# Pair 3's transposes moved from TensorE to the DMA crossbar, and the loads held differently

## The chip, the cores and the metric

The kernel runs on one core of one Trainium2 chip. A core has five engines that run their own instruction streams and wait for each other through semaphores: TensorE (PE, matmuls, with its weight loads listed apart as PEld), VectorE (DVE), ScalarE (ACT), GpSimd (POOL) and SyncE (SP), and 16 DMA engines that move data between memory and the core. The metric is device time in microseconds for one execution; lower is better. Six runs of the kernel before gave 228.18 to 228.51 us, median 228.28 us.

## The reference: what is computed

A gated recurrence over 768 tokens for 4 batches and 8 heads of width 64, followed by a feed-forward layer with a sigmoid gate:

```python
gamma = 1.0 - 2.0 ** (-5.0 - np.arange(H))
scale = 1.0 / np.sqrt(D)
for t in range(S):
    state = gamma[None, :, None, None] * state + np.einsum('bhd,bhe->bhde', k[:, :, t], v[:, :, t])
    y[:, :, t] = scale * np.einsum('bhd,bhde->bhe', q[:, :, t], state)
x = y.transpose(0, 2, 1, 3).reshape(B * S, H * D)          # 3072 x 512
gate = 1.0 / (1.0 + np.exp(-(x @ w_gate)))                 # d_ff 1536
out = gate * (x @ w_val) @ w_out                           # 3072 x 512
```

## The kernel before

**Tiles and stages.** The recurrence is computed in chunks of C = 128 tokens. There are NT = 6 chunks; the four batches of a chunk are treated as two *pairs* of batches, so there are 12 pairs, numbered i = 2t + h for chunk t and batch half h. Pairs 0 and 1 (chunk 0) form the start of the kernel and have code of their own (`first_...`). For a later pair the steps are:

- `load_kq(i)` (L69): k and q of the pair come as bf16 into tiles `kn[i]` and `qn[i]`, three DMA issues each (L63 once, L67 twice: the second batch has its heads swapped two by two). `load_v(i)` (L54) brings `vs[i]` in one issue (L57). All of these are issued by POOL and converted from float32 on the way. `load_next(i)` (L488) is `load_kq` and `load_v`, seven issues.
- k and q must stand with the head width on the partitions for the score matmuls. This is done in one of two ways. `transpose(i, j)` (L203) transposes eight 128x128 blocks on PE into a bank of PSUM (L207) and has ACT copy them to the tile `kqT[i]` (L208); j is the batch of the pair. `xbar(i)` (L210) has SP issue two transposing DMAs, one for k and one for q (L213), into a tile of the tag `kqX` (four buffers). The kernel before transposes pairs 2 and 3 on PE and pairs 4 to 11 by the DMA crossbar.
- `scale_k(i)` (L216, L218): POOL multiplies `kn[i]` by a table of decays, giving `ks[i]`.
- `scores` (L226), `mask` (L232, DVE, with the table `maskk`), `inter` (L242: the old state times q), `intra` (L249: the masked scores times v), `y_out` (L265, DVE, into `xT[t]`, the input of the feed-forward layer), `state` (L272: `ks` times v), `state_sum` (L281) and `casts` (L285). `block(old, new)` (L287) does `inter`, `intra` and `y_out` of one pair and `scores`, `state` and `mask` of the next.

The feed-forward layer works on a chunk's 512 tokens: `up` (L386) has PE compute a gate part and a value part (L364), ACT takes the sigmoid (L382) and DVE the product (L383); `down` (L394) has PE multiply with `wo` (L399), ACT copy the result (L403) and SP issue the output's DMA (L404), 256 KB for each of the four batches of a chunk.

**What sets the order.** The schedule is written out by hand: each engine's queue takes its instructions in the order in which the program states them, and only semaphores hold them back. An instruction of an engine therefore waits behind everything that the program gave to this engine earlier. Chunk 0's feed-forward layer is written out (L468 to L521), with pair 2's and part of pair 3's steps between its parts. For t = 1 to 5 the loop at L542 goes through the groups of `up` and `down` of that chunk (20 groups: in chunk 1 six groups for each half of the tokens, then eight groups of `down`; in chunks 2 to 5 twelve of `up` and eight of `down`), and after a group does the steps that the dictionary `plan` (L530) names for it. A step `(4, xbar, 4)` under 1 is done after group 4 of chunk 1.

**The hold.** `hold(i)` (L527, L528) has POOL copy one element of pair i's transposed q into a small tile. The result is used by nobody; the copy makes POOL wait for the crossbar transfer of q, and so everything that POOL does after it, loads above all, comes after that transfer.

**The constants.** `last_constants` (L174) has DVE make a 0/1 mask in `causal`; `later_tables` (L177) has POOL build `tabsk` (L182, four copies) and `maskk` (L184, two products), which `scale_k` and `mask` need.

Of the kernel before, what the change touches and what calls it, by code (L numbers as in the profile page):

```python
# [9 lines left out]
BF16 = mybir.dt.bfloat16  # L10
# [5 lines left out]
def kernel(  # L16
# [12 lines left out]
    nc = tc.nc  # L29
# [3 lines left out]
    C = 128  # L33
    NT = S // C
    NP = H // 2
# [7 lines left out]
    const = ctx.enter_context(tc.tile_pool(name="const", bufs=1))  # L43
# [6 lines left out]
    kn, qn, ks, vs, kqT = {}, {}, {}, {}, {}  # L50
# [3 lines left out]
    def load_v(i):  # L54
        t, h = divmod(i, 2)
        vs[i] = ld.tile([C, 2 * H, D], BF16, tag="vs", name="vs", bufs=6)
        nc.gpsimd.dma_start(out=vs[i], in_=v[2 * h:2 * h + 2, :, t * C:(t + 1) * C, :].rearrange("b h s d -> s (b h) d"))  # L57
# [11 lines left out]
    def load_kq(i):  # L69
        load_swapped(kn, k, i, "kn", 6)  # L70
        load_swapped(qn, q, i, "qn", 4)
# [13 lines left out]
    def load_out(s):  # L85
        nc.gpsimd.dma_start(out=wo[:, s * 3:(s + 1) * 3, :],
                            in_=moe_w_out.rearrange("(n p) d -> p n d", p=128)[:, s * 3:(s + 1) * 3, :])
# [86 lines left out]
    def last_constants():  # L174
        nc.vector.tensor_scalar(causal, ahead, 0.0, None, op0=ALU.is_le)

    def later_tables():  # L177
        src = tabs.rearrange("s (p e) t -> s e t p", e=2)
        dst = tabsk.rearrange("s t j (p e) -> s j e t p", e=2)
        for j in range(2):  # L180
            for e in range(2):
                nc.gpsimd.tensor_copy(dst[:, j, e], src[:, e ^ j])  # L182
        for e in range(2):
            nc.gpsimd.tensor_tensor(maskk[:, e], causal.unsqueeze(1).to_broadcast([128, NP, C]),  # L184
                                    tabsk[:, 0, e, 0::2].unsqueeze(2).to_broadcast([128, NP, C]), op=ALU.mult)
# [5 lines left out]
    def bank(shape, dt=F32):  # L191
        return pf.tile(shape, dt, tag="ff", name="ff")

    def half(e):
        return slice(e * D, (e + 1) * D)

    def heads(t, j, p):
        return t[:, j * H + 2 * p:j * H + 2 * p + 2, :].rearrange("s h d -> s (h d)")

    def new_kqT(i):  # L200
        kqT[i] = at.tile([128, 2, 2, NP, C], BF16, tag="kqT", name="kqT", bufs=2)

    def transpose(i, j):  # L203
        tp = bank([128, 2, NP, C], BF16)
        for which, x in enumerate((kn[i], qn[i])):
            for p in range(NP):
                nc.tensor.transpose(tp[:, which, p, :], heads(x, j, p), ident)  # L207
        nc.scalar.copy(kqT[i][:, :, j], tp)  # L208

    def xbar(i):  # L210
        kqT[i] = at.tile([128, 2, 2, NP, C], BF16, tag="kqX", name="kqX", bufs=4)
        for which, x in enumerate((kn[i], qn[i])):
            nc.sync.dma_start_transpose(out=kqT[i][:, which].rearrange("d j p s -> d (j p) s"),  # L213
                                        in_=x.rearrange("s h d -> s (h d)"))

    def scale_k(i):  # L216
        ks[i] = ld.tile([C, 2 * H, D], BF16, tag="ks", name="ks", bufs=3)
        nc.gpsimd.tensor_tensor(ks[i], kn[i], tabsk[:, i // 2].rearrange("s j h -> s (j h)").unsqueeze(2)  # L218
                                .to_broadcast([C, 2 * H, D]), op=ALU.mult)
# [14 lines left out]
    def new_y(i):  # L234
        for j in range(2):
            y[i, j] = bank([128, NP, C])
# [19 lines left out]
    def x_of(t, kk, lo=0, hi=512):  # L256
        per = NP // len(xT[t])
        return xT[t][kk // per][:, kk % per, lo:hi]
# [17 lines left out]
    def new_za(i):  # L276
        za[i] = at.tile([128, 2, NP, D], F32, tag="za", name="za", bufs=4)
# [5 lines left out]
    def casts(i):  # L283
        zb[i] = at.tile([128, 2, NP, D], BF16, tag="zb", name="zb", bufs=4)
        nc.vector.tensor_tensor(zb[i], za[i], tabz[:, i // 2 + 1].unsqueeze(3).to_broadcast([128, 2, NP, D]), op=ALU.mult)  # L285
# [58 lines left out]
    def first_state(i):  # L344
        z = bank([128, 2, NP, D])
        for j in range(2):
            for p in range(NP):
                for e in range(2):
                    n = j * H + 2 * p + e
                    nc.tensor.matmul(z[half(e ^ j), j, p, :], ks[i][:, n, :], vs[i][:, n, :],  # L350
                                     start=(j == 0 and p == 0), stop=True, skip_group_check=True)
        new_za(i)
        nc.vector.tensor_copy(za[i], z)
# [5 lines left out]
    def up_part(t, w, n1s, lo=0, hi=512):  # L359
        n = hi - lo  # L360
        u = bank([128, 512])
        for i, n1 in enumerate(n1s):
            for kk in range(KT):
                nc.tensor.matmul(u[:, i * n:(i + 1) * n], w[:, kk, n1 * 128:(n1 + 1) * 128], x_of(t, kk, lo, hi),  # L364
                                 start=(kk == 0), stop=(kk == KT - 1))
        return u[:, :len(n1s) * n]
# [9 lines left out]
    def gate_times_val(t, n1s, lo, hi, ps):  # L376
        n = hi - lo
        if t not in hT:
            hT[t] = ffn.tile([128, NFF, 512], BF16, tag="hT", name="hT", bufs=2)
        gs = ffn.tile([128, 512], F32, tag="gs", name="gs")  # L380
        g = gs[:, :len(n1s) * n]
        nc.scalar.activation(g, ps[0], AX.Sigmoid)  # L382
        nc.vector.tensor_tensor(hT[t][:, n1s[0]:n1s[-1] + 1, lo:hi], g.rearrange("p (i n) -> p i n", n=n),  # L383
                                ps[1].rearrange("p (i n) -> p i n", n=n), op=ALU.mult)
# [6 lines left out]
    def rows(t, b):  # L391
        return b * S + t * C

    def down(t, b, lo, hi):  # L394
        if lo == 0:
            po[b] = bank([128, 512])
        o = po[b]
        for n1 in range(lo, hi):
            nc.tensor.matmul(o, hT[t][:, n1, b * C:(b + 1) * C], wo[:, n1, :], start=(n1 == 0), stop=(n1 == NFF - 1))  # L399
        if hi < NFF:  # L400
            return
        ob = ffn.tile([128, D_MODEL], F32, tag="ob", name="ob")
        nc.scalar.copy(ob, o)  # L403
        nc.sync.dma_start(out=out[rows(t, b):rows(t, b) + C, :], in_=ob)  # L404
# [65 lines left out]
    for n1 in (2, 4):  # L470
        gates = [up_part(0, wg, (n1 + i,)) for i in range(2)]
        for i in range(2):
            gate_times_val(0, (n1 + i,), 0, 512, (gates[i], up_part(0, wv, (n1 + i,))))
        first_state(n1 // 2 - 1)
    last_constants()
    load_out(0)
    load_out(1)
    load_kq(2)
    load_out(2)
    later_tables()  # L480
    load_out(3)
    load_v(2)
    casts(0)
# [4 lines left out]
    def load_next(i):  # L488
        load_kq(i)
        load_v(i)  # L490

    load_next(3)
    scale_k(2)
    new_kqT(2)
# [10 lines left out]
        mask(2, j, 1)  # L505
    for b in range(3):
        down(0, b, 9, 12)
    load_next(4)
    down(0, 3, 0, 6)
    new_y(2)  # L510
    inter(2)
# [5 lines left out]
    state_sum(2)  # L517
    down(0, 3, 6, 12)
    casts(2)
    new_kqT(3)  # L520
    transpose(3, 0)  # L521

    held = const.tile([128, 1], BF16, name="held")

    def hold(i):  # L527
        nc.gpsimd.tensor_copy(held, kqT[i][:, 1, 1, NP - 1, C - 1:C])  # L528

    plan = {  # L530
        1: [(0, transpose, 3, 1), (0, scale_k, 3), (0, load_next, 5), (2, block, None, 3), (4, block, 3, None),
            (4, xbar, 4), (4, scale_k, 4), (4, hold, 4), (4, load_next, 6), (5, casts, 3), (7, xbar, 5), (7, scale_k, 5),
            (7, hold, 5), (7, load_next, 7), (11, block, None, 4), (12, casts, 4), (12, xbar, 6), (12, scale_k, 6),
            (12, hold, 6), (12, load_next, 8), (14, block, 4, 5), (16, casts, 5), (18, block, 5, 6), (19, casts, 6)],
        2: [(0, xbar, 7), (0, scale_k, 7), (0, hold, 7), (0, load_next, 9), (8, block, 6, 7), (10, casts, 7), (10, xbar, 8),
            (10, scale_k, 8), (10, hold, 8), (10, load_next, 10), (17, block, 7, 8), (19, casts, 8)],
        3: [(2, xbar, 9), (2, scale_k, 9), (2, hold, 9), (2, load_next, 11), (8, block, 8, 9), (10, casts, 9),
            (10, xbar, 10), (17, block, 9, 10)],
        4: [(2, xbar, 11), (8, block, 10, 11), (17, block, 11, None)],
        5: [],  # L540
    }
# [42 lines left out]
```

## Time and profile before

| What | us |
|---|---|
| Median of six runs | 228.28 |
| Time of the profiled execution | 228.26 |
| Its span, first to last instruction | 226.5 |
| PE busy | 220.6 (97% of the span) |
| DVE busy | 112.1 (50%) |
| POOL busy | 105.2 (46%) |
| ACT busy | 72.1 (32%) |
| Transposes on PE, L207, 32 of them in four groups of eight | 3.0 busy, 219 ns each |
| ACT's copies of them, L208, four | 4.1, 1014 ns each |
| `scale_k`, L218, eight | 15.9, 1993 ns each |
| `later_tables`, L182 and L184 | 0.7 and 2.0 |
| `hold`, L528, six | 1.2 busy, 26.8 idle ahead of them |
| Crossbar transfers, k / q, issue to landing, median | 3.9 / 3.4 |

How to read it: the profile is one execution on the chip, with every instruction's start and duration. Busy times of different engines overlap, so they don't add up to the span. Matmuls on PE overlap each other, so their listed durations add up to more than PE's time; the chain that ended last counts each stretch once. That chain is found by going back from the last instruction, at each step to what released it. The time of an execution is 1.8 us longer than the span (228.26 against 226.5).

### The profile page before, as it was taken

The page shows a single profiled execution, that of the slowest core. Times are in us where ns is not written, and L with a number is a line of the kernel's source. Part 1 is how long each engine was busy: PE and PEld are TensorE (multiplying, and loading weights), DVE is VectorE, ACT ScalarE, POOL GpSimd, SP SyncE. Part 2 cuts the span into 40 slices and gives each one's busy share as a digit, 9 for nine tenths or more (in the row PEclk, how much of TensorE's full clock was granted, in tenths as well). Part 3 has the DMA queues.
Part 4 walks back from the last instruction along what each step waited for, and adds up shares of the span by engine and source line. Part 5 has one row for each costly group of instructions (what it writes and reads, how often), then busy time and mean ns, then how long its engine had stood idle before and what let it go on. Part 6 is the DMA issues. An engine that isn't in the chain of part 4 may idle for free.

```text
span 226.5 us, 4343 instructions
## 1 busy us (share of the span) xinstructions
PE 220.6 (97%) x1774; PEld 116.8 (52%) x1774; DVE 112.1 (50%) x199; ACT 72.1 (32%) x123; POOL 105.2 (46%) x127
## 2 busy tenths in 40 slices
PE   7799999999999999999999999999999999999994
PEld 2444444558888555445445445445445444444443
DVE  7753653163953779645906534905443802333301
ACT  6683333236233112332321342321433321333221
POOL 8999959999979987099800091000000000000000
PEclk9999999999999999999999999999999999999999
DMA  9999999999999999999921799012600012100022
GB/s 132 149 177 193 189 190 163 166 235 183 163 152 151 141 175 187 188 126 101 105 76 70 169 126 80 0 46 96 140 0 0 3 46 96 48 0 0 0 96 93
DMA packets 103668, 25.19 MB, mean 111 GB/s; under 512 B 92640, under 2 KB 100704, under 8 KB 103648
## 3 DMA queue, kind: packets, MB, share of 16 engines
q0 software_dynamic: 80928, 13.90, 81.7%
q1 hardware_dynamic: 21536, 10.69, 19.9%
q10 hardware_dynamic: 1184, 0.33, 0.6%
q8 instruction: 14, 0.23, 0.4%
q14 instruction: 6, 0.05, 0.1%
HBM read 28.31 MB, written 6.29 MB: 153 GB/s over the span
## 4 chain that ended last, share of the span: by engine, by line
PE 94%; DMA 2%; POOL 1%; DVE 1%; issue 0%; ACT 0%; POOLq 0%
PE ff L364 54%; PE ff L399 27%; PE ff L226 3%; PE ff L249 3%; DMA kn<-in_k_dram 2%; PE ff L373 2%; PE ff L242 2%; PE ff L412 1%; PE ff L272 1%; PE ff L426 1%; PE ff L207 1%; DVE st L326 1%; PE ff L336 0%; POOL kn L92 0%; POOL qn L92 0%; PE ff L319 0%
## 5 line engine op out<-in xcount | busy, mean ns | idle before, releaser
L383 DVE TENSOR_TENSOR hT<-gs,ff 128x512 bf16<-128x512 f32 x72 | 49.0, 686 | 63.1 <-PE ff L364 59.7
L364 PE MATMUL ff<-xT,wg 128*128 128x512 bf16 (+1 forms) x328 | 71.7, 348 | 0.0
L364 PE MATMUL ff<-xT,wv 128*128 128x512 bf16 (+1 forms) x328 | 71.7, 348 | 0.0
L382 ACT ACTIVATE gs<-ff 128x512 f32<-128x512 f32 x72 | 42.9, 597 | 82.7 <-PE ff L364 80.2
L399 PE MATMUL ff<-wo,hT 128*128 128x512 bf16 x276 | 62.1, 379 | 0.0
L364 PEld LDWEIGHTS <-wv 128*128 128x128 bf16 x328 | 32.1, 98 | 28.5
L364 PEld LDWEIGHTS <-wg 128*128 128x128 bf16 x328 | 31.4, 98 | 27.6
L399 PEld LDWEIGHTS <-hT 128*128 128x128 bf16 x276 | 26.3, 98 | 30.7
L403 ACT COPY ob<-ff 128x512 f32<-128x512 f32 x23 | 13.5, 585 | 58.7 <-PE ff L399 55.2
L232 DVE TENSOR_TENSOR st<-ff,maskk 128x512 bf16<-128x512 f32 x40 | 24.8, 681 | 6.4 <-PE ff L226 6.4
L265 DVE TENSOR_TENSOR xT<-ff,taby 128x512 bf16<-128x512 f32 x20 | 12.9, 686 | 28.8 <-PE ff L249 28.8
L218 POOL TENSOR_TENSOR ks<-kn,tabsk 128x1024 bf16<-128x1024 bf16 x8 | 15.9, 1993 | 0.0
L67 POOL DMA_DIRECT2D qn<-in_q_dram x20 | 15.4, 797 | 0.8 <-DMA wv<-in_moe_w_val_dram 0.6
L67 POOL DMA_DIRECT2D kn<-in_k_dram x20 | 15.2, 778 | 0.0
L528 POOL COPY held<-kqX 128x1 bf16<-128x1 bf16 x6 | 1.2, 194 | 26.8 <-DMA kqX<-qn 26.7
L57 POOL DMA_DIRECT2D vs<-in_v_dram x10 | 12.2, 1217 | 0.0
L63 POOL DMA_DIRECT2D kn<-in_k_dram x10 | 9.4, 944 | 1.2 <-issue 1.1
L63 POOL DMA_DIRECT2D qn<-in_q_dram x10 | 9.3, 929 | 0.0
L285 DVE TENSOR_TENSOR zb<-za,tabz 128x512 bf16<-128x512 f32 x10 | 9.2, 925 | 0.2
L426 PE MATMUL ff<-zero 128*128 128x512 bf16 x22 | 7.6, 464 | 1.2 <-DVE zero L135 1.2
L249 PE MATMUL ff<-st,vs 128*64 128x128 bf16 x160 | 6.4, 222 | 0.0
L326 DVE TENSOR_TENSOR st<-ff,decay 128x512 bf16<-128x512 f32 x8 | 5.2, 686 | 1.7 <-ACT kqT L320 0.9
(73 smaller groups left out, 121.5 us busy)
## 6 DMA issues: line engine op xcount, KB each, us to landing
out_dram<-ob SPq DMA_DIRECT2D x23, 256.0 KB, 2.1
vs<-in_v_dram POOLq DMA_DIRECT2D x10, 256.0 KB, 6.3
kn<-in_k_dram POOLq DMA_DIRECT2D x13, 128.0 KB, 5.0
qn<-in_q_dram POOLq DMA_DIRECT2D x13, 128.0 KB, 5.0
wo<-in_moe_w_out_dram POOLq DMA_DIRECT2D x4, 384.0 KB, 7.8
wg<-in_moe_w_gate_dram POOLq DMA_DIRECT2D x5, 256.0 KB, 6.0
wv<-in_moe_w_val_dram POOLq DMA_DIRECT2D x5, 256.0 KB, 6.5
kn<-in_k_dram POOLq DMA_DIRECT2D x20, 64.0 KB, 5.4
```

What stands on the lines that cost most here:

```text
L57: nc.gpsimd.dma_start(out=vs[i], in_=v[2 * h:2 * h + 2, :, t * C:(t + 1) * C, :].rearrange("b h s d -> s (b h) d"))
L63: nc.gpsimd.dma_start(out=tiles[i][:, 0:H], in_=src[0])
L67: nc.gpsimd.dma_start(out=dst[:, e], in_=pairs[:, 1 - e])
L218: nc.gpsimd.tensor_tensor(ks[i], kn[i], tabsk[:, i // 2].rearrange("s j h -> s (j h)").unsqueeze(2) .to_broadcast([C, 2 * H, D]), op=ALU.mult)
L232: nc.vector.tensor_tensor(st[i, j], sc[i, j][e], maskk[:, e ^ j], op=ALU.mult)
L249: nc.tensor.matmul(y[i, j][half(e), p, :], vs[i][:, j * H + 2 * p + e, :], st[:, p, :], start=False, stop=True, skip_group_check=True)
L265: nc.vector.tensor_tensor(xT[t][0][:, :, c:c + C], y[i, j], taby, op=ALU.mult)
L364: nc.tensor.matmul(u[:, i * n:(i + 1) * n], w[:, kk, n1 * 128:(n1 + 1) * 128], x_of(t, kk, lo, hi), start=(kk == 0), stop=(kk == KT - 1))
L382: nc.scalar.activation(g, ps[0], AX.Sigmoid)
L383: nc.vector.tensor_tensor(hT[t][:, n1s[0]:n1s[-1] + 1, lo:hi], g.rearrange("p (i n) -> p i n", n=n), ps[1].rearrange("p (i n) -> p i n", n ...
L399: nc.tensor.matmul(o, hT[t][:, n1, b * C:(b + 1) * C], wo[:, n1, :], start=(n1 == 0), stop=(n1 == NFF - 1))
L403: nc.scalar.copy(ob, o)
```

## The change

Pair 3 is transposed by `xbar(3)` in place of `transpose(3, 0)` and `transpose(3, 1)`. `xbar(3)`, `scale_k(3)` and `hold(3)` are stated after the third part of `down(0, 0..2)` and ahead of `load_next(4)`; `load_next(5)` follows at once. `hold(5)` is gone. From pair 6 on each load is stated one hold later than before: pair 7's after `hold(6)` (before: after `hold(5)`), 8's after `hold(7)`, 9's after `hold(8)`, 10's after `hold(9)`, 11's after a new `hold(10)` (before: after `hold(9)`). `last_constants` and `later_tables` are stated earlier: after the third and fourth gate-times-value products of chunk 0 and before the state of pair 0, so ahead of `load_out(0)`, `load_out(1)`, `load_kq(2)` and `load_out(2)`. The definition of `hold` moves up.

```diff
         for i in range(2):
             gate_times_val(0, (n1 + i,), 0, 512, (gates[i], up_part(0, wv, (n1 + i,))))
+        if n1 == 2:
+            last_constants()
+            later_tables()
         first_state(n1 // 2 - 1)
-    last_constants()
     load_out(0)
     load_out(1)
     load_kq(2)
     load_out(2)
-    later_tables()
     load_out(3)
     load_v(2)
...
     for b in range(3):
         down(0, b, 9, 12)
+    xbar(3)
+    scale_k(3)
+    hold(3)
     load_next(4)
+    load_next(5)
     down(0, 3, 0, 6)
...
     casts(2)
-    new_kqT(3)
-    transpose(3, 0)
...
     plan = {
-        1: [(0, transpose, 3, 1), (0, scale_k, 3), (0, load_next, 5), (2, block, None, 3), (4, block, 3, None),
-            (4, xbar, 4), (4, scale_k, 4), (4, hold, 4), (4, load_next, 6), (5, casts, 3), (7, xbar, 5), (7, scale_k, 5),
-            (7, hold, 5), (7, load_next, 7), (11, block, None, 4), (12, casts, 4), (12, xbar, 6), (12, scale_k, 6),
-            (12, hold, 6), (12, load_next, 8), (14, block, 4, 5), (16, casts, 5), (18, block, 5, 6), (19, casts, 6)],
-        2: [(0, xbar, 7), (0, scale_k, 7), (0, hold, 7), (0, load_next, 9), (8, block, 6, 7), (10, casts, 7), (10, xbar, 8),
-            (10, scale_k, 8), (10, hold, 8), (10, load_next, 10), (17, block, 7, 8), (19, casts, 8)],
-        3: [(2, xbar, 9), (2, scale_k, 9), (2, hold, 9), (2, load_next, 11), (8, block, 8, 9), (10, casts, 9),
-            (10, xbar, 10), (17, block, 9, 10)],
+        1: [(2, block, None, 3), (4, block, 3, None), (4, xbar, 4), (4, scale_k, 4), (4, hold, 4), (4, load_next, 6),
+            (5, casts, 3), (7, xbar, 5), (7, scale_k, 5), (11, block, None, 4), (12, casts, 4), (12, xbar, 6), (12, scale_k, 6),
+            (12, hold, 6), (12, load_next, 7), (14, block, 4, 5), (16, casts, 5), (18, block, 5, 6), (19, casts, 6)],
+        2: [(0, xbar, 7), (0, scale_k, 7), (0, hold, 7), (0, load_next, 8), (8, block, 6, 7), (10, casts, 7), (10, xbar, 8),
+            (10, scale_k, 8), (10, hold, 8), (10, load_next, 9), (17, block, 7, 8), (19, casts, 8)],
+        3: [(2, xbar, 9), (2, scale_k, 9), (2, hold, 9), (2, load_next, 10), (8, block, 8, 9), (10, casts, 9),
+            (10, xbar, 10), (10, hold, 10), (10, load_next, 11), (17, block, 9, 10)],
```

More of the change, by code (lines that the diff above doesn't have):

```diff
@@ L490, in load_next, with hold @@
         load_v(i)
+    held = const.tile([128, 1], BF16, name="held")
+    def hold(i):
+        nc.gpsimd.tensor_copy(held, kqT[i][:, 1, 1, NP - 1, C - 1:C])
     load_next(3)
@@ L519 @@
     casts(2)
-    new_kqT(3)
-    transpose(3, 0)
-    held = const.tile([128, 1], BF16, name="held")
-    def hold(i):
-        nc.gpsimd.tensor_copy(held, kqT[i][:, 1, 1, NP - 1, C - 1:C])
-    plan = {
-        1: [(0, transpose, 3, 1), (0, scale_k, 3), (0, load_next, 5), (2, block, None, 3), (4, block, 3, None),
-            (4, xbar, 4), (4, scale_k, 4), (4, hold, 4), (4, load_next, 6), (5, casts, 3), (7, xbar, 5), (7, scale_k, 5),
-            (7, hold, 5), (7, load_next, 7), (11, block, None, 4), (12, casts, 4), (12, xbar, 6), (12, scale_k, 6),
-            (12, hold, 6), (12, load_next, 8), (14, block, 4, 5), (16, casts, 5), (18, block, 5, 6), (19, casts, 6)],
-        2: [(0, xbar, 7), (0, scale_k, 7), (0, hold, 7), (0, load_next, 9), (8, block, 6, 7), (10, casts, 7), (10, xbar, 8),
-            (10, scale_k, 8), (10, hold, 8), (10, load_next, 10), (17, block, 7, 8), (19, casts, 8)],
-        3: [(2, xbar, 9), (2, scale_k, 9), (2, hold, 9), (2, load_next, 11), (8, block, 8, 9), (10, casts, 9),
-            (10, xbar, 10), (17, block, 9, 10)],
+    plan = {
+        1: [(2, block, None, 3), (4, block, 3, None), (4, xbar, 4), (4, scale_k, 4), (4, hold, 4), (4, load_next, 6),
[5 more added lines that the diff above has]
+            (10, xbar, 10), (10, hold, 10), (10, load_next, 11), (17, block, 9, 10)],
         4: [(2, xbar, 11), (8, block, 10, 11), (17, block, 11, None)],
```

## The prediction

> **What bounds the kernel now.** First the busy shares, then the chain of work that ended last, then the queues that feed it. The page's busy time, granted clock and DMA rows:
>
> ```profile
> PE 220.6 (97%) x1774; PEld 116.8 (52%) x1774; DVE 112.1 (50%) x199; ACT 72.1 (32%) x123; POOL 105.2 (46%) x127
> PEclk9999999999999999999999999999999999999999
> DMA  9999999999999999999921799012600012100022
> ```
>
> PE is 97% busy at full granted clock; the 16 DMA engines are full for the first half. In every stretch between 20 and 200 us PE is busy for the whole of it, and the chain in order of time (start us, us, what) is PE alone from 12.2 us to 223.4:
>
> ```profile
> 48.97 1.40 PE ff L399 x6
> 50.37 0.45 PE ff L207 x8
> 50.82 1.75 PE ff L364 x16
> 52.57 0.45 PE ff L207 x8
> 53.01 3.49 PE ff L364 x32
> 56.51 0.55 PE ff L226 x16
> ...
> 79.54 0.55 PE ff L226 x16
> ...
> 80.66 0.25 PE ff L272 x16
> ...
> 86.55 0.55 PE ff L226 x16
> ```
>
> So any PE instruction taken away shortens the run by its share of this chain, as long as nothing PE needs comes later than PE. The two L207 rows are pair 3's transposes; 56.51, 79.54 and 86.55 are the scores of pairs 3, 5 and 6, 80.66 the state of pair 5.
>
> POOL's timeline (start, us, line, operation), where all loads are issued:
>
> ```profile
> 34.18 0.70 POOL L182 COPY tabsk<-tabs 128x24 f32<-128x24 f32 x4
> 34.86 2.04 POOL L184 TENSOR_TENSOR maskk<-causal,tabsk 128x512 f32<-128x512 f32 x2
> ...
> 46.53 0.96 POOL L63 DMA_DIRECT2D kn<-in_k_dram  x1
> ...
> 63.84 0.18 POOL L528 COPY held<-kqX 128x1 bf16<-128x1 bf16 x1 [1.61 <-DMA kqX<-qn]
> 64.07 0.95 POOL L63 DMA_DIRECT2D kn<-in_k_dram  x1
> ...
> 70.00 1.98 POOL L218 TENSOR_TENSOR ks<-kn,tabsk 128x1024 bf16<-128x1024 bf16 x1
> ```
>
> A hold ends when the crossbar transfer lands, and the next pair's loads start 0.2 us later. SP's timeline, and two answers on DMA issues (the last number is us from issue to landing; the q transfers issued at 56.38 and 95.37):
>
> ```profile
> 45.86 5.58 SPq L404 DMA_DIRECT2D out_dram<-ob  x4
> 53.98 1.33 SPq L213 DMA_TRANSPOSE kqX<-kn  x1
> 56.38 1.45 SPq L213 DMA_TRANSPOSE kqX<-qn  x1
> ```
> ```profile
> kqX<-qn SPq DMA_TRANSPOSE x1, 7.4
> ```
> ```profile
> kqX<-qn SPq DMA_TRANSPOSE x1, 3.2
> ```
>
> A crossbar transfer takes 7.4 us with other pairs' loads in flight and 3.2 with none: that spread is the unknown of this change.
>
> **1. Removed: 16 PE transposes and two copies of ACT.** The chain gives pair 3's two groups 0.45 us (50.37 to 50.82) and 0.44 (52.57 to 53.01): 0.89 us, all on the path. ACT's two 1.01 us copies (L208) were beside it (ACT 32% busy): nothing.
>
> The Trainium skill ("TensorE: Matmul & The Clock Gate", Part 4: PE-mode transpose) states about 275 ns for a 128x128 bf16 transpose inside a kernel; by it the 16 would be worth 4.4 us, and the time would be about 223.9. Here a transpose also shows 219 ns from start to end, but eight in a row hold the chain for 0.45 us, 56 ns each, so the trace decides for the small sum. A second rule speaks against the change: "VectorE: DVE Perf Modes" (Rules for kernel authors) says to use TensorE for a 128x128 transpose where PSUM will do, and its table of transpose paths has the crossbar at 1309 ns against 390. That compares latencies of one block; this chain is bound by PE.
>
> What stood behind pair 3's first transposes now starts at 50.37: the first gate matmuls of t=1, which read what `y_out(2)` wrote. That row of DVE:
>
> ```profile
> 48.54 1.29 DVE L265 TENSOR_TENSOR xT<-ff,taby 128x512 bf16<-128x512 f32 x2 [1.71 <-PE ff L249]
> ```
>
> It ends at 49.83, 0.54 us ahead. Cost nothing; if that margin were gone, at most 0.45 us come back. ACT's copy of down(0,3) waited until 50.49 for an output transfer; without pair 4's loads beside it this lands no later.
>
> **2. Moved: tables ahead of nine DMA issues.** `later_tables` (0.70 + 2.04 = 2.7 us of POOL) goes in front of both `load_out` calls, `load_kq(2)`'s six loads and `load_out(2)`. Its `causal` is a 0.22 us DVE step that now ends near 23.5, before POOL is there at 24.5. Pair 2's loads then issue 2.7 us later. When they land is another matter: the first `wo` load, issued at 24.49, took 8.7 us against 5.4 for the last one, so some 3.3 us of work stood ahead of it, more than the pause. POOL also waited 0.22 + 0.58 + 1.83 us in this stretch; the last two ended 0.3 us after the transfer eight issues earlier had landed (30.55, 33.19), and those waits shrink by what is spent sooner. I take 0 for the shift in landing. Bounds: 0 to 2.7 us. q of pair 2 for the first half landed at 28.36 + 9.4 = 37.8 and PE loads it at 38.49: 0.7 us margin, so at worst PE stalls 2.0. Pair 3's loads then end some 1.3 us earlier on POOL (44.7 before).
>
> **3. Added: pair 3's crossbar transfer.** On SP it stands behind the outputs of down(0,0..2). Their three copies end on ACT at 45.25 + 1.88 = 47.1; one output issue is 0.33 us; so k issues at 47.5 and q, 1.40 us later (as 93.97 to 95.37), at 48.9. q of pair 3 landed at 42.8 + 5.4 = 48.2 even before the move. Landing: 3.2 to 7.4 us after issue, 52.1 to 56.3. Pair 4's loads are held, but three outputs of 256 KB are in flight, so I take 4.1 (as an output takes among loads of one pair): 53.0. Scores of pair 3 need it at 56.51 - 0.89 = 55.6: margin 2.6, stall at the upper end 0.7. Output (0,3), behind it on SP, is ready at 51.1, when q's issue is done (50.2). `scale_k(3)`, 2.0 us, now comes before pair 4's loads, near 45.3 on POOL, with its k landed by 46.2 at the latest: nothing.
>
> **4. Added wait: POOL holds pair 4's and 5's loads until then.** Pair 4 starts at 53.2 instead of 46.53, and with it a chain behind the hold on POOL: load 4 (6.2 us of issues), load 5 (6.1), `scale_k(4)` 2.0, hold(4), load 6 (6.0), `scale_k(5)` 2.0. From a load's start to its q transfer's issue the rows have 9.9, 11.0 and 9.6 us (pairs 4, 5, 6); for pair 8, with no transfer beside it, its last q load landed after 8.7. With T the landing of pair 3:
> - pair 4: T + 0.2 + 8.7, landing 7.0 us later beside load 5: T + 15.9 = 68.9. Needed at 74.28 - 0.89 = 73.4.
> - load 6 starts T + 16.2; `scale_k(5)` ends 8 us later, T + 24.2 = 77.2. Needed by pair 5's state at 79.8.
> - pair 5 (load starts T + 6.4; 9.6; 6.6 landing): T + 22.6 = 75.6. Needed at 78.65.
> - pair 6 (T + 16.2 + 9.6 + 4.4): T + 30.2 = 83.2. Needed at 85.7.
> All hidden, by 2.5 us or more. With the worst rows (11.0, 7.4) `scale_k(5)` ends at T + 27.
>
> **5. From pair 6 on, loads one hold later.** Load 7 starts near 83.5, lands by 93.2, and its transfer goes after output (1,3) (90.0 before), landing by 97; needed at 104.3. Load 8 at 97, landed transfer 110, needed 119.1. Load 9 at 110, pair 9's transfer behind the outputs near 125 as before. Load 10 at 129.3, transfer landed 141.5, needed 153.8; load 11 at 142, landed by 152, its transfer behind the outputs near 159 as before. Covered by 7 us or more; on the DMA engines this is the empty half.
>
> **Sum.** 228.26 (profiled execution, span 226.5 and 1.8 around it) - 0.89 = 227.37; it stands 0.02 below the median of 228.28, so 227.4.
>
> **Rivals.**
> - Slower: POOL's chain makes pair 5 late. It starts to cost when T + 24.2 (worst rows T + 27) passes 79.8, and the run is slower than before by over 0.2% once that stall passes 1.35 us, T above 54.1 with the worst rows. With T = 56.3 as well, ks of pair 5 is ready at 83.3: stall 3.5 us, 230.9. For it: 7.4 us has been seen, and before nothing stood between pair 5's loads and its scaling. Against: the hold clears the DMA engines for just this transfer. 0.11.
> - Slower: pair 2 lands late because the tables are issued first: 227.4 + 2.0 = 229.4 at worst. Against: the backlog. 0.06.
> - Same: pair 3's transfer itself lands last at its scores (T near 56.3): 228.1. Moderate delays of the other two also end here. 0.11.
> - The early gate matmuls catch on `y_out(2)` and half the gain does not come: 227.8. 0.05.
> - Forecast, no stall that counts: 227.4, own range 227.2 to 227.8. 0.67.
>
> **How the numbers follow.** 0.2% (0.46 us) is about what a measurement of this kernel tells from none. Faster: the forecast and a part of the fourth, 0.69. Same: 0.14. Slower: 0.17. The range reaches from 227.2 through the same cases to a stall of 1.3 us, 228.7.
>
> **What would show it.** No L207 group after 42 us; chain again PE alone, with gate matmuls at 50.4 and pair 3's scores near 55.6; a held row near 53 on POOL; pair 2's transposes at 38.5 with no wait; scaling of pair 5 done by 79. Wrong would be a wait of PE on kqX, ks or kn in the waits, or any non-PE piece in the chain between 37 and 90 us.

## The result, and the profile after

The changed kernel takes 227.55 us (median of 20 runs) against 228.34 us (42 runs of the kernel before): ratio 0.9967, 95% interval 0.9959 to 0.9975, so 0.57 to 0.94 us faster. The prediction was 227.4 us, range 227.2 to 228.7. Runs more than 1.5% above the fastest of their kernel, here one of the 20 at 231.41 us, count as slow ones and are left out of the ratios. The profiled execution took 227.43 us, its span 225.7 (before: 228.26 and 226.5).

The page's busy time, granted clock and DMA rows of the changed kernel:

```profile
PE 220.3 (98%) x1758; PEld 116.7 (52%) x1758; DVE 114.4 (51%) x199; ACT 70.3 (31%) x121; POOL 105.4 (47%) x128
...
PEclk9999999999999999999999999999999999999999
DMA  9999999997999999979999699795600012100022
```

PE has 16 instructions less and ACT two. The DMA row (5.6 us to a slice) dips near 53 us, where pair 4's loads are held, and stays busy up to 150 where it was nearly idle from 113 to 125 before: the loads are spread instead of pushed ahead. The chain in order of time (start us, us, what):

```profile
48.85 0.25 PE ff L272 x16
49.10 1.40 PE ff L399 x6
50.50 5.24 PE ff L364 x48
55.74 0.55 PE ff L226 x16
...
78.78 0.55 PE ff L226 x16
...
79.90 0.25 PE ff L272 x16
...
85.83 0.55 PE ff L226 x16
```

Where two L207 groups stood, 48 gate and value matmuls now run in one piece. This execution reaches the end of chunk 0's last part of down, at 50.50, 0.13 us later than the profiled one of before (start-up, ahead of anything the change touches on PE), and pair 3's scores at 55.74, 0.77 earlier: 0.90 us came out between the two. From there the chain is PE alone, as before, to 222.63, 0.72 before the time at which it ended in the profile of before (223.35).

POOL's timeline of the changed kernel (start, us, line, operation, idle before it and what ended it):

```profile
24.50 0.74 POOL L182 COPY tabsk<-tabs 128x24 f32<-128x24 f32 x4
25.17 2.06 POOL L184 TENSOR_TENSOR maskk<-causal,tabsk 128x512 f32<-128x512 f32 x2
...
53.41 0.19 POOL L496 COPY held<-kqX 128x1 bf16<-128x1 bf16 x1 [5.37 <-DMA kqX<-qn]
...
70.01 0.18 POOL L496 COPY held<-kqX 128x1 bf16<-128x1 bf16 x1 [2.55 <-DMA kqX<-qn]
...
76.38 3.84 POOL L218 TENSOR_TENSOR ks<-kn,tabsk 128x1024 bf16<-128x1024 bf16 x2
84.45 0.19 POOL L496 COPY held<-kqX 128x1 bf16<-128x1 bf16 x1 [4.23 <-DMA kqX<-qn]
```

and SP's (q's transfers of pairs 3, 4, 5 and 6):

```profile
49.25 1.94 SPq L213 DMA_TRANSPOSE kqX<-qn  x1
...
62.08 1.25 SPq L213 DMA_TRANSPOSE kqX<-qn  x1
...
70.69 1.23 SPq L213 DMA_TRANSPOSE kqX<-qn  x1
...
79.45 1.28 SPq L213 DMA_TRANSPOSE kqX<-qn  x1
```

By the answers on DMA issues they landed after 4.1, 7.8, 6.3 and 4.9 us: at 53.4, 69.9, 77.0 and 84.4. The scores stand at 55.7, 73.5, 78.8 and 85.8, so the margins are 2.4, 3.6, 1.8 and 1.4 us. Pair 5's scaling ends at about 78.3, 1.6 ahead of its state. The gain is whole in this execution; what is thin is its cover.

### The profile page after: what moved, and what is told of

The parts are those of the page before. It is cut to its first block, busy times and chain, and to the rows that moved or that the text cites. A ratio compares the mean times of both kernels' runs of the same rounds, so it can differ in the third digit from the quotient of the medians.

```text
span 225.7 us, 4323 instructions
## 1 busy us (share of the span) xinstructions
PE 220.3 (98%) x1758; PEld 116.7 (52%) x1758; DVE 114.4 (51%) x199; ACT 70.3 (31%) x121; POOL 105.4 (47%) x128
## 4 chain that ended last, share of the span: by engine, by line
PE 97%; DVE 1%; ACT 1%; issue 0%
PE ff L364 54%; PE ff L399 27%; PE ff L226 3%; PE ff L426 3%; PE ff L249 3%; PE ff L373 2%; PE ff L242 2%; PE ff L412 1%; PE ff L272 1%; ACT kqT L320 1%; PE ff L319 1%; DVE st L326 1%; PE ff L336 0%; PE ff L207 0%; PE ff L350 0%
## 5 line engine op out<-in xcount | busy, mean ns | idle before, releaser
L383 DVE TENSOR_TENSOR hT<-gs,ff 128x512 bf16<-128x512 f32 x72 | 48.9, 686 | 60.7 <-PE ff L364 57.2
L496 POOL COPY held<-kqX 128x1 bf16<-128x1 bf16 x7 | 1.3, 184 | 38.2 <-DMA kqX<-qn 38.2
L285 DVE TENSOR_TENSOR zb<-za,tabz 128x512 bf16<-128x512 f32 x10 | 11.5, 1158 | 0.2
L426 PE MATMUL ff<-zero 128*128 128x512 bf16 x22 | 8.4, 507 | 1.2 <-DVE zero L135 1.2
L79 POOL DMA_DIRECT2D wg<-in_moe_w_gate_dram x7 | 5.7, 831 | 0.0
```

Source lines behind the costliest of these rows:

```text
L426: nc.tensor.matmul(u, zero[:, :128], zero, start=True, stop=True)
```

## The experiments

The theory to be tried was that of the prediction: PE bounds the kernel, the change takes 0.89 us from it, and everything else is hidden. All ratios are to the kernel before, run on the same chip; a microsecond figure behind a ratio is the ratio's difference from one times 228.5.

**Is the gain the PE time?** The transposes were put back on PE at their old places, beside the crossbar transfer that is used.

```diff
     casts(2)
+    unused_transpose(3, 0)     # as transpose, but ACT copies one column to a spare tile
...
-        1: [(2, block, None, 3), ...
+        1: [(0, unused_transpose, 3, 1), (2, block, None, 3), ...
```

> The changed kernel, with pair 3's 16 transposes put back on PE at their old places, their result unused but for one column that ACT copies; pair 3 still comes through the crossbar. My theory: the 0.89 us come back, 228.4 us, two L207-like groups of 0.45 us in the chain. Rival (the gain is due to loads that are placed better): it stays at 227.5 us.

Ratio 0.9997 (0.9988 to 1.0007): the gain is gone. The chain of that kernel holds them again, 0.45 us each:

```profile
50.63 0.45 PE ff L535 x8
51.08 1.75 PE ff L364 x16
52.82 0.45 PE ff L535 x8
53.27 3.49 PE ff L364 x32
```

So with all of the new load order in place, these 16 instructions (and two copies of one column on ACT) alone make the difference between a gain and none.

**The tables alone.** The kernel before, with `last_constants` and `later_tables` at their new place and nothing else changed:

```diff
+        if n1 == 2:
+            last_constants()
+            later_tables()
         first_state(n1 // 2 - 1)
-    last_constants()
...
-    later_tables()
```

> The kernel before with one edit: the tables are built ahead of the output weights' and pair 2's loads. My theory (the change's gain is the 0.89 us of PE time alone, everything else is hidden): no difference from before, 228.3 us within 0.2; pair 2's q for the first half lands near 37.8 as before, though it is issued 2.7 us later. Rival (the order of the early loads moves time): pair 2 lands up to 2.7 us later, PE waits up to 2.0 us at its transposes near 38.5, up to 230.3 us.

Ratio 0.9992 (0.9981 to 1.0003): no difference. Pair 2's q for the first half was issued at 31.11, 2.7 us later than before, and landed after 7.1 us instead of 9.4, at 38.2 against 37.8. The backlog in front of it hid all but some 0.4 us of the pause, PE waited for none of it, and that rival falls.

**The tables left late in the changed kernel.** The opposite edit: everything of the change but this.

```diff
-        if n1 == 2:
-            last_constants()
-            later_tables()
         first_state(n1 // 2 - 1)
+    last_constants()
...
     load_out(2)
+    later_tables()
```

> The changed kernel with the tables built late again, behind pair 2's loads and the third output-weight load, as before the change. My theory (moving the tables is worth nothing by itself: pair 3's q, landed at 47.5 or 48.2, is transposed from 49 on in either case, behind three outputs): 227.5 us, the hold of pair 3 ends within 0.5 us of 53.4. Rival (pair 3's loads, ending 1.3 us later, are then in flight beside the transfer): q of pair 3 takes 5 us or more, the hold ends near 54.5 and pairs 5 and 6 are late by some 0.3 us, 227.8 us or more with more spread.

Ratio 0.9996 (0.9980 to 1.0012): all of the gain is gone, which I had not expected. Its twelve runs lie between 227.50 and 229.23 us; the profiled execution, at 229.17, is one of the longest, so its trace shows how the gain is lost, not what an average run loses. POOL and SP of that kernel:

```profile
47.90 1.89 POOL L218 TENSOR_TENSOR ks<-kn,tabsk 128x1024 bf16<-128x1024 bf16 x1 [1.47 <-DMA kn<-in_k_dram]
55.75 0.19 POOL L495 COPY held<-kqX 128x1 bf16<-128x1 bf16 x1 [5.95 <-DMA kqX<-qn]
```
```profile
49.49 4.23 SPq L213 DMA_TRANSPOSE kqX<-qn  x1
...
73.54 2.07 SPq L213 DMA_TRANSPOSE kqX<-qn  x1
```

and PE's waits (engine, line, releaser: total us, times, longest):

```profile
PE ff L226 <- DMA kqX<-qn: 1.5, 1, 1.5
```

Pair 3's loads land 1.4 to 2.0 us later than in the changed kernel (the last of q at 48.9 against 47.5, v at 50.8 against 48.8) and are still in flight when its transfer starts: POOL's scaling waits for k until 47.9, q's transfer needs 4.2 us on SP instead of 1.9 and lands after 6.2 instead of 4.1. The hold ends at 55.7 instead of 53.4. Pair 3's scores are still in time (no wait there), but everything behind the hold is 2.3 us later, and pair 5's transfer lands at 80.3 for scores at 78.8: the wait of 1.5 us. Moving the tables is worth nothing by itself; as cover for the transfer it is worth 0.6 to 0.7 us by the ratios.

**The hold of pair 3 left out.**

```diff
     scale_k(3)
-    hold(3)
     load_next(4)
```

> The changed kernel without the hold of pair 3: pair 4's and 5's loads follow the scaling of pair 3 at once, near 48 us, beside the crossbar transfer. My theory: q of pair 3 takes 5.8 to 7.4 us instead of 4.1 and lands at 55.0 to 56.6 where its scores want it at 55.74; between nothing and 0.9 us is lost, 227.5 to 228.4 us. Rival (the hold does nothing): landing after 4.1 us, 227.5 us; and pairs 4 to 6 come 5 us earlier, so if their margins are what makes some executions of the changed kernel longer, this one varies less.

Ratio 1.0033 (1.0018 to 1.0048), 0.75 us slower than before. Right in kind, too small in size: pair 4's loads start at 48.7, q takes 7.7 us and lands at 57.5 for scores wanted at 55.9. The chain of that kernel:

```profile
49.75 7.71 DMA kqX<-qn
57.46 0.14 issue
57.59 0.62 PE ff L226 x16
```

PE waits 1.7 us there. The rival that the hold does nothing falls. Its other half, that this kernel would vary less, did not come true either (228.60 to 230.40 us), but with a wait of its own at pair 3 that settles nothing.

**The crossbar transfer alone.** The kernel before with pair 3 through the crossbar and no other edit, so pair 4's loads run ahead of it and beside it:

```diff
         down(0, b, 9, 12)
+    xbar(3)
     load_next(4)
...
-    new_kqT(3)
-    transpose(3, 0)
...
-        1: [(0, transpose, 3, 1), (0, scale_k, 3), ...
+        1: [(0, scale_k, 3), ...
```

> The kernel before with pair 3 through the crossbar (issued at the same place as in the changed kernel) and nothing else: tables late, pair 4's loads from 46.5 us on ahead of and beside the transfer, no hold of pair 3. My theory: the 0.89 us of PE are gained and up to 0.9 lost to a late transfer of pair 3 (landing 6 to 7.5 us after its issue near 49): 227.5 to 228.4 us. Rival (the holding and the reordering are needed for any gain): 228.3 us or more, with PE waiting at pair 3's scores for more than 0.9 us.

Ratio 1.0244 (1.0218 to 1.0269), 5.6 us slower: my theory (227.5 to 228.4 us) failed, and the rival, that the holding and the reordering are needed for any gain, holds. The transfer took 9.2 us from q's issue; PE's timeline of that kernel:

```profile
59.81 0.86 PE L226 MATMUL ff<-kqX 64*128 64x128 bf16 x16 [3.83 <-DMA kqX<-qn]
60.60 0.64 PE L272 MATMUL ff<-vs,ks 128*64 128x64 bf16 x16
61.17 1.89 PE L364 MATMUL ff<-xT,wg 128*128 128x256 bf16 x8
62.85 1.34 PE L364 MATMUL ff<-xT,wv 128*128 128x256 bf16 x8
64.03 1.04 PE L364 MATMUL ff<-xT,wg 128*128 128x256 bf16 x8
```

and a stretch of its windows (from:to, us, busy of PE, PEld, DVE, ACT, POOL, then granted clock, DMA share, GB/s):

```profile
60.00:66.00 6.00, 6.00 (x72) 4.64 (x70) 3.77 (x6) 1.19 (x2) 2.79 (x2) 0.72 1.90 157
```

The wait of 3.8 us is not the whole cost: after it the granted clock is 0.72 over six microseconds, and the same eight gate matmuls take 1.89 us where they take 1.04 a little later. In the chain the scores, the state and the 32 gate and value matmuls up to 65.94 take 6.1 us, against 4.5 in the changed kernel: another 1.6 us. (This execution, 233.10 us, is the fastest of the five.)

**How far the hold's chain can be pushed.** Two POOL products of 1.9 us, result unused, between the hold and pair 4's loads:

```diff
     hold(3)
+    spare = const.tile([C, 2 * H, D], BF16, name="spare")
+    for _ in range(2):
+        nc.gpsimd.tensor_tensor(spare, kn[3], ..., op=ALU.mult)
     load_next(4)
```

> The changed kernel with two more POOL products of 1.9 us each (result unused) between the hold of pair 3 and pair 4's loads, so the chain behind the hold starts 3.8 us later. In the changed kernel's trace pair 6's transposed q lands at 84.4 and its scores stand at 85.8, pair 5's scaling ends at 78.3 and its state stands at 79.9. My theory (margins of 1.4 to 1.8 us at pairs 5 and 6 are what the hold's chain has left): a stall of 2.0 to 2.4 us, 229.5 to 230 us, the first wait of PE at pair 5, and none at pair 3. Rival (the chain is well hidden, margins as I predicted of 2.5 us or more, or contention gets less with the delay): a stall of 1.3 us or less, 228.8 us or less.

Ratio 1.0126 (1.0083 to 1.0169), 2.9 us slower than before and some 3.6 slower than the changed kernel: more than my 2.0 to 2.4. Its runs lie between 230.45 and 234.66 us. The long wait is where I put it, at pair 5 (another 0.4 us is at pair 4), and the clock adds to it again; PE's waits and a stretch of the windows:

```profile
PE ff L226 <- DMA kqX<-qn: 2.8, 2, 2.4
```
```profile
80.00:92.00 12.00, 10.40 (x139) 6.30 (x140) 5.93 (x10) 1.17 (x2) 7.58 (x9) 0.86 1.64 159
```

By the chains, pair 5's scores and what stands behind them, up to the next 24 output matmuls, take 8.2 us instead of 6.7: another 1.5 us. With the waits of 2.8 that is the 4.3 us by which this execution (231.73) is longer than the changed kernel's.

The Trainium skill ("TensorE: Matmul & The Clock Gate", Part 1: The HAM clock gate) gives a window of about 3.4 us without work before the clock is halved. Here it fell after a wait of 2.4 us, and not after one of 1.7 (1.00 from 40 to 65 us in the kernel without the hold); the measurement goes first. These two waits do not make a threshold: two more runs of this kernel, at 230.45 and 230.64 us, are 3 us longer than the changed kernel and show a granted clock of 1.00.

**The later loads as before the change.** Pair 5's hold back, pair 7's loads after it, each later load one hold earlier:

```diff
-            ... (7, xbar, 5), (7, scale_k, 5), (11, block, None, 4), ... (12, hold, 6), (12, load_next, 7), ...
+            ... (7, xbar, 5), (7, scale_k, 5), (7, hold, 5), (7, load_next, 7), (11, block, None, 4), ...
+            (12, hold, 6), (12, load_next, 8), ...
...                                          # and so on to pair 11
```

> The changed kernel with the later loads as in the kernel before: hold of pair 5 back, pair 7's loads after it, 8's after the hold of pair 6 and so on. My theory (the last part of the change keeps load 7 off the crossbar transfer of pair 6, whose margin is 1.4 us): pair 6's q takes 6.3 to 7.2 us instead of 4.9 and lands 0 to 1 us after its scores want it: 227.6 to 228.6 us, with a wait of PE at pair 6's scores. Rival (as I predicted, that part is hidden and worth nothing): 227.5 us.

Ratio 0.9992 (0.9975 to 1.0010): the gain is lost here too, and three of the twelve runs took 231.4 to 231.8 us. Why is not settled. The chain of the profiled execution (229.04 us) and PE's waits in it:

```profile
71.66 8.18 DMA kqX<-qn
...
86.39 1.94 POOL ks L218
88.33 0.04 issue
88.38 0.44 PE ff L272 x16
```
```profile
PE ff L226 <- DMA kqX<-qn: 1.4, 1, 1.4
...
PE ff L272 <- POOL ks L218: 0.2, 1, 0.2
```

The two waits, 1.4 and 0.2 us, are the 1.6 us by which this execution is longer than the changed kernel's. The first can hardly be the work of the edit: pair 5's transfer took 8.2 us and made its scores wait until 79.98, before load 7 began at 80.4. Up to that point the two kernels give SP the same instructions in the same order, and POOL too up to the end of pair 5's scaling. So this is also a picture of what can happen in the changed kernel. The second is the edit's: with the old order pair 6's scaling is queued on POOL behind load 7 and ends at 88.3; in the changed kernel it runs right behind pair 5's and ends at 80.2, for a state at 86.95. Had pair 5's hold ended with the scaling ahead of it (78.7), load 7 would, by my estimate, have taken POOL to 84.9 and pair 6's scaling to 86.9: just in time. So the old order leaves pair 6's state no margin where the new one leaves 6.7 us; here it cost 0.2.

Pair 6's own transfer, which I had expected to be late, was waited for by nobody. That does not clear it: it took 6.1 us instead of 4.9 and landed at 86.7, in time only because the wait at pair 5 had moved its scores to 86.98; the changed kernel has them at 85.83. An execution without the first wait might wait here, by some 0.9 us, as I expected. No profile of one was taken, so which of the three loses the gain in most runs stays open.

**Why the changed kernel varies.** Its runs, but for the one at 231.41, lie between 227.2 and 228.5 us, with about a third above 227.8. The middle half of them spans 0.6 us, that of the 42 runs of the kernel before 0.3; but the kernel before has single long runs too, up to 1.2 us above its fastest. Three kernels were to show whether the thin margins are the cause. Once more the changed kernel:

> The changed kernel once more, beside the two below on one chip. Theory (margins of 1.4 to 1.8 us at pairs 5 and 6 that some executions use up): median 227.3 to 227.7 us, about one execution in three above 227.8. Rival (the spread of its first runs was of that chip): all within 0.3 us of each other.

Ratio 0.9970 (0.9959 to 0.9981), 227.50 to 228.50 us, five of twelve above 227.8: the spread came again. How much of it belongs to the change is less clear, since the kernel before ran from 228.12 to 229.36 us there. Pair 3's transfer after the first output instead of the third:

```diff
     for b in range(3):
         down(0, b, 9, 12)
-    xbar(3)
+        if b == 0:
+            xbar(3)
```

> The changed kernel with pair 3's crossbar transfer issued after the first output of chunk 0 instead of after the third. My theory (some executions of the changed kernel are 0.5 to 1 us longer because a margin of 1.4 to 2.4 us is used up): the transfer of q is issued near 47.8 instead of 49.25 and the hold ends 1.2 us or more earlier; all margins behind it grow by as much, median 227.3 us, few executions above 227.8. Rival (the spread comes from elsewhere): median 227.5 us and the same spread.

Ratio 0.9952 (0.9938 to 0.9967), all five runs from 227.33 to 227.71, as my theory had it; so it was run again, beside the changed kernel:

> Once more the changed kernel with pair 3's transfer after the first output of chunk 0. Theory (half a microsecond or more of margin added at pairs 5 and 6): median 227.3 to 227.5 us and no execution above 227.8, so 0 to 0.3 us below the changed kernel. Rival (the small spread of its first five executions was chance): the same spread as the changed kernel.

Ratio 0.9968 (0.9955 to 0.9980), 227.32 to 228.63 us, seven of twelve above 227.8. The first five were chance. The edit also gave little of what it was for: q went out 1.3 us earlier, but the hold ended at 52.8 and 53.0 instead of 53.4. The last kernel adds to it that v is loaded after k and q:

```diff
-    load_next(4)
-    load_next(5)
+    load_kq(4)
+    load_kq(5)
+    load_v(4)
+    load_v(5)
...
-            (4, load_next, 6), ... (7, scale_k, 5), ...
+            (4, load_kq, 6), ... (7, scale_k, 5), (7, load_v, 6), ...
```

> The changed kernel with pair 3's transfer after the first output and v's loads moved back: k and q of pairs 4 and 5 are loaded first and their v after, and v of pair 6 after the scaling of pair 5. In profiled executions of the changed kernel pair 5's q lands 1.1 to 1.8 us ahead of its scores, at 77.0 to 77.8. My theory (the longer executions are those in which pair 5 uses up this margin): pair 5's q is issued 1.2 us earlier on POOL, lands near 75.5 to 76.5 and leaves 2.3 us or more: median 227.3 to 227.5 us and no execution above 227.9. Rival (the longer executions have another cause): median 227.6 to 227.8 and a third of the executions above 227.8, as without this edit.

Ratio 0.9953 (0.9936 to 0.9970), six runs from 227.34 to 227.91 us, so one above 227.8. But its trace does not show the margin I had counted on. Pair 5's q on SP's timeline, and the answer on that DMA issue:

```profile
68.89 2.03 SPq L213 DMA_TRANSPOSE kqX<-qn  x1
```
```profile
kqX<-qn SPq DMA_TRANSPOSE x1, 7.9
```

Pair 5's q went out 1.8 us earlier and took 7.9 us instead of 6.3: 76.8, against 77.0 in the changed kernel. The intervals of this kernel and of the changed one overlap, and after what happened with the earlier transfer six quiet runs prove nothing. That the long executions of the changed kernel wait at pair 5 is argued from the run with the old later loads; no profile of a long execution of the changed kernel itself was caught, so it stays open. The record has one more hint: the run of 231.41 us shows a granted clock of 0.992, where the other 19 have 0.998 to 1.000 and the two profiled executions with PE waits of 2.4 and 3.8 us have 0.993 and 0.991. Without a profile of it that proves no wait.

**Pair 2 through the crossbar as well.** On top of the earlier transfer:

```diff
     load_out(0)
-    load_out(1)
     load_kq(2)
+    load_out(1)
...
-    new_kqT(2)
-    ... transpose(2, 0) ... transpose(2, 1) ...
+    xbar(2)
+    for lo in (0, 3, 6):
+        for b in range(3):
+            down(0, b, lo, lo + 3)
```

> As the run with pair 3's transfer after the first output, and pair 2 through the crossbar as well: its loads go ahead of the second output-weight load, its PE transposes are left out, chunk 0's down is done in steps of three. My theory (each pair is worth 0.89 us of PE time as long as its transfer lands in time): PE wants pair 2's scores at 43.2; its q is issued near 37 and takes 4 to 7.5 us beside pair 3's loads, so it lands between 41 and 44.5: 226.5 us if in time, 227.8 with a stall of 1.3. Rival (the transfer beside loads is late by more than 0.9 us, or the second weight load is): no gain, 227.5 us or more.

Ratio 1.0243 (1.0218 to 1.0269), 5.6 us slower. The transfer ran beside two output-weight loads and pair 3's loads; those can't be held, since pair 3 is wanted 12 us later. The chain of that kernel:

```profile
36.95 11.10 DMA kqX<-qn
48.05 0.14 issue
48.19 1.04 PE ff L226 x16
```

11.1 us, the longest of all, a PE wait of 4.5 us and a slowed clock behind it (the scores and the next 15 output matmuls took 6.8 us; in the changed kernel they take 3.9); PE also waited 0.4 us for an output weight. The rival had it.

## Why the prediction was right, point by point

- *Removed, 0.89 us, all on the path.* Right: 0.90 us came out between 50.5 and 55.7, and putting the transposes back takes the whole gain away. The early gate matmuls did not catch on `y_out(2)`: they start right behind down's last part, at 50.50, with `y_out(2)` done at 49.96.
- *Tables moved, shift in landing 0.* Right for the kernel as changed (q of pair 2 landed at 31.12 + 6.4 = 37.5) and nearly for the edit alone (0.4 us later). But I mentioned the 1.3 us that pair 3's loads win (0.8 on POOL, as measured: 43.9 against 44.7) only in passing and gave it no value, by the reasoning that its q was there at 48.2 in any case. With the tables late, the tail of these loads is beside the transfer, and the gain is gone.
- *Pair 3 lands at 53.0, in time for 55.6.* Right: 53.4 for 55.7. The 4.1 us were borrowed from another kind of transfer, an output; in the five profiles with the tables early, the hold in place and the transfer after the third output it took 3.8 to 4.2 us, so the value was no accident of one run, but why an output's landing should stand for it was not shown. Wrong was the upper end of the unknown: I took 7.4 us, the longest landing in the trace of before, as the bound. In the changed kernel itself pair 4's took 7.8, and other transfers that met loads took 7.7, 8.2, 9.2 and 11.1 us; where my worst stall at pair 3 was 0.7 us, the wait was 1.7 without the hold and, with pair 4's loads ahead, 3.8.
- *The chain behind the hold, margins of 2.5 us or more.* Mis-sized: predicted 68.9, 75.6 and 83.2 for the transfers of pairs 4, 5 and 6 and 77.2 for pair 5's scaling, measured 69.9, 77.0, 84.4 and 78.3, each 1.0 to 1.4 us later. Of this 0.4 is the landing of pair 3, the rest longer landings beside other loads: pair 4's transfer took 7.8 us where I had 7.0, and pair 5's went out at 70.7 where my terms put it at 69.0. The margins are 1.4 to 1.8 us at pairs 5 and 6. The slower rival, this chain overtaking pair 5, is the one that was nearest: PE waited at pair 5 in the profiles of three experiments. But what it waited for was the transfer at the scores, not the scaling at the state that the rival named.
- *From pair 6 on, covered by 7 us or more.* No wait there, but less cover: pair 7's hold ended at 98.5 for scores at 104.5, 6 us, and pair 8's at 112.5 for 119.3. What I missed is that this part also takes pair 6's scaling out from behind load 7 and load 7 out from beside pair 6's transfer. With the old order the gain was lost, and how much of that these two did is open.
- *The sum, 227.4.* Measured 227.55; the profiled execution's 227.43 is within 0.1 of the sum. Between it and the median stand the longer executions, for which the prediction had no term in its time, only in its range.

## What to carry to other kernels

On PE, busy throughout in this kernel, taking instructions away was worth their share of the chain, and this could be read off beforehand to within 0.2 us; the work is in showing that nothing comes later than before. The edits around such a change may be what pays for it: three of them (the tables, the hold of pair 3, the later loads) lost the whole gain when undone singly, and the tables, the one also tried alone, were then worth nothing. A landing time from a trace is the landing time in that traffic; for a transfer that will meet other loads, the longest one seen is no upper bound. A late one can cost more than its wait: behind waits of 2.4, 3.8 and 4.5 us the slowed clock took another 1.5, 1.6 and 2.9.

## What the runs showed that was not expected

- A crossbar transfer of 128 x 1024 elements took from 3.1 us with no loads beside it to 11.1 us among loads; its issue on SP itself stretched with it, from 1.2 to 4.5 us.
- In the profiles, the granted clock fell after PE waits of 2.4, 3.8 and 4.5 us (0.86 over twelve, 0.72 over six and 0.77 over fifteen microseconds around them) and not after 1.4 to 1.7.
- Issuing a transfer earlier did not land it as much earlier: 1.3 us on SP became 0.3 to 0.6 at the hold, 1.8 became 0.2 at pair 5.
